# Two more tiles' first products by seven block products, and one table of steps for the whole program

## The chip, the core and the metric

The kernel runs on one core of a Trainium2 chip. The metric is the time of one execution on the device in microseconds (us); lower is better. Engines: PE (matmul; PEld is its weight load), DVE, ACT, POOL, and SP, which here issues all DMAs.

## What is computed

Attention with a window of 128 over 8 batches of 576 tokens and 8 heads, and on its output a dense GELU block:

```python
scores = q @ k.T / sqrt(64) + bias            # bias: -slope * |i - j|
scores = where((0 <= i - j) & (i - j < 128), scores, -1e9)
attn = softmax(scores) @ v                    # 8 x 8 x 576 x 64
x = attn as 4608 x 512
h = x @ w_in                                  # 512 x 2048
g = 0.5 * h * (1 + erf(h / sqrt(2)))
out = g @ w_out                               # 2048 x 512
```

All arrays are float32.

## The kernel before, in words

**Products.** Nearly every float32 operand is split into a high and a low float16 part, and a product is three float16 products (high-high, low-high, high-low). The 4608 tokens are nine tiles of 512. A tile needs its *first product* (h, from x and w_in), GELU, and its *second product* (from g and w_out).

**Plain form.** `mlp_in` (L845) makes h of a tile in 16 banks of PSUM, each by 12 products of 128x128 weights and 512 columns: 192 in all. `mlp_out` (L892; L889 for tile 0, in float32) does as much for the output.

**Block form.** x, w_in and h are seen as two by two blocks, and seven block products of half size (p1 to p7) take the place of eight; some of them use sums of blocks of x (xs) and of w_in (t). With `d` from 0 to 3 for four pieces of 512 features, each piece takes 7 x 12 products of 256 columns: 336 a tile. `Middle` (L1205) does so for tiles 4, 5 and 6, `Seven` (L1093) for tile 8. Both collect the products in two banks, u and v; between products ACT copies u out and DVE adds v to the copy, and GELU follows. `seven_out` (L1302) makes the second products of tiles 7 and 8 in block form too, by sums of g (slots, made in `Sums`) and of w_out (L1318).

**Sums of the weights.** `store_sums` (L982, step K) makes the sums of w_in in eight groups: six POOL ops, a cast by ACT, a low part by DVE, a store to memory (`stored`). It works in the buffers ld_0 and ld_1, which also take q and k of each batch. `load_middle` (L1183) and `load_sums` (L1004) load them again, 1 MB for each piece. `sums_of_weights_out` (L1011, steps P0 to P2, and piece 3 in tile 7) makes the sums of w_out on DVE and ACT into qbuf, kbuf, vbuf and e_main, after attention is done with these.

**Sums of x.** `sums_of_middle` (L1173, step Z) makes them half on POOL and half on DVE.

**Order of the work.** Each function is a generator that issues one or a few instructions at each step. Two tables written out as text set the order for all engines: `ORDER` for batches 0 to 2 and tiles 0 and 1, and after it `LATER` up to tile 6. An engine runs its instructions in that order and waits where an operand isn't ready. Letters name the work: s, S scores; M, N softmax; w, W, y, Y products with v; H and 1 to 7 first products; o, O second products; q, v splitting of q, k and v; a digit ahead is the tile. Tables of bank numbers choose PSUM banks. Between the two tables the pools of PSUM and of the output buffers are closed and opened anew (L1477). Tiles 7 and 8 stand behind the tables as a plain loop (L1531).

**The beginning.** Batch 0's attention is exact float32: scores, softmax on ACT from PSUM, `turn` (PE transposes, L711), `turned` (ACT copies, L719), `weigh` (L798), `leave` (x of tile 0, L818). Beside it ACT and DVE put together and split w_in (`magnitude_in`, `join_in`, `split_in`: L338, L345, L360), and ACT passes once over v for its largest value (`stat_v`, L484), which the scale of x needs.

```python
IN = (4, 5, 6, 8)
...
    with tc.manual_schedule(engines=None):
        for step in ORDER.split():
            next(tasks[step])
...
    early.close()
...
        for step in LATER.split():
            next(later[step])
    for t in range(FAST_OUT, NTILE):
...
        if t == FAST:
            seven_all(t, places)
```

## Time and profile before

| | |
|---|---|
| median of 3 runs | 866.54 us (866.50 to 867.53) |
| profiled execution | 866.36 us |
| its span, first to last instruction | 864.6 us |
| busy PE, DVE, ACT, POOL | 848.4, 696.0, 627.7, 296.9 us |
| mean granted clock of PE | 0.998 |

The span is what the views of the trace cover; about 1.8 us of the execution lie around it. Busy times are of one engine each and overlap. Matmuls are pipelined: the mean of one is longer than the distance from one to the next, which is read from how long a row of them takes.

### The profile page before, as it was taken

What the parts mean: (1) busy time and instruction counts of PE and PEld (TensorE: products, weight loads), DVE (VectorE), ACT (ScalarE), POOL (GpSimd) and SP (SyncE); (2) the same over time, 40 slices, a digit from 0 to 9 for tenths busy, and PEclk for the clock granted to TensorE, in tenths of its full rate; (3) what the DMA queues carried; (4) which work ended last, traced back from release to release, by engine and by line L of the source; (5) the groups of instructions that cost most, each with busy time, mean ns of one, the idle gap of its engine ahead of it and who ended that gap; (6) DMA issues with size and microseconds to landing.
All of it is one profiled execution on the core that took longest, in us unless ns stands there. A gap on an engine that the chain in (4) does not pass through costs nothing.

```text
span 864.6 us, 18999 instructions
## 1 busy us (share of the span) xinstructions
PE 848.4 (98%) x7572; PEld 520.5 (60%) x7572; DVE 696.0 (81%) x1258; ACT 627.7 (73%) x1236; POOL 296.9 (34%) x481
## 2 busy tenths in 40 slices
PE   6999999999999999999999999999999999999998
PEld 4654445544554455445478647865686554588887
DVE  6999999999887865988586989799968899922861
ACT  7999879897678967796579595968596647713850
POOL 2011000123056972879624555547244510000000
PEclk9999999999999999999999999999999999999999
DMA  9865844644542468324943566266712630111201
GB/s 310 278 198 185 291 121 109 161 130 90 124 116 62 105 143 194 98 68 142 231 160 103 186 141 208 81 196 147 213 50 55 119 97 1 49 62 38 98 2 50
DMA packets 178057, 112.64 MB, mean 130 GB/s; under 512 B 134064, under 2 KB 156720, under 8 KB 175792
## 3 DMA queue, kind: packets, MB, share of 16 engines
q1 hardware_dynamic: 177968, 111.43, 44.8%
q8 instruction: 59, 0.97, 0.5%
q14 instruction: 30, 0.25, 0.1%
HBM read 63.31 MB, written 13.63 MB: 89 GB/s over the span
## 4 chain that ended last, share of the span: by engine, by line
PE 75%; DVE 13%; ACT 4%; DMA 4%; issue 3%; POOL 1%; SPq 0%; ACTq 0%; DVEq 0%; POOLq 0%
PE o L892 28%; PE h L845 13%; PE u L1216 7%; PE v L1216 5%; PE av L798 4%; PE u_out L1318 4%; PE sc L617 4%; PE u L1114 2%; PE v L1114 2%; PE z_out L1318 1%; PE x_out L1318 1%; PE y_out L1318 1%; PE v_out L1318 1%; DMA q<-qp 1%; DVE nmax L726 1%
## 5 line engine op out<-in xcount | busy, mean ns | idle before, releaser
L845 PE MATMUL h<-x,wi 128*128 128x512 f16 x960 | 211.2, 379 | 2.1 <-ACT g L866 1.5
L892 PE MATMUL o<-wo,g 128*128 128x512 f16 x864 | 192.2, 379 | 0.0
L892 PEld LDWEIGHTS <-g 128*128 128x128 f16 x1152 | 110.6, 98 | 131.4 <-issue 0.3
L845 PEld LDWEIGHTS <-wi 128*128 128x128 f16 x960 | 92.9, 98 | 115.9 <-issue 5.3
L730 ACT ACTIVATE s<-s,nmax 128x192 f32<-128x192 f32 x252 | 111.5, 444 | 27.3 <-DVE nmax L726 25.3
L740 POOL TENSOR_SCALAR s<-s,z 128x192 f32<-128x192 f32 x180 | 96.0, 554 | 39.2 <-DVE z L734 23.7
L643 DVE SCALAR_TENSOR_TENSOR s<-sc,cs,bias_h 128x384 f32<-128x384 f32 x112 | 67.1, 607 | 3.1 <-PE sc L617 2.7
L649 POOL MEMSET s<- 64x128 f32 (+1 forms) x112 | 19.3, 174 | 143.4 <-DVE s L643 116.4
L892 PE MATMUL o<-wo_first,g 128*128 128x512 f16 x288 | 66.0, 379 | 0.0
L1216 PEld LDWEIGHTS <-t 128*128 128x128 f16 x576 | 56.1, 98 | 6.9
L726 DVE TENSOR_REDUCE nmax<-s 128x5 f32<-128x960 f32 (+1 forms) x56 | 58.1, 1043 | 1.2 <-POOL s L649 1.0
L870 POOL TENSOR_SCALAR g<-g,sg 128x512 f16<-128x512 f32 x48 | 41.4, 871 | 49.8 <-DMA q<-qp 26.6
L749 DVE TENSOR_TENSOR e_main<-s,e_main 128x960 f16<-128x960 f32 (+1 forms) x40 | 46.1, 1158 | 14.8 <-ACT e_main L742 14.5
L889 PE MATMUL o<-zo,g 128*128 128x512 f32 x128 | 57.0, 597 | 0.0
L617 PE MATMUL sc<-kbuf,qbuf 64*64 64x192 f16 (+3 forms) x1656 | 48.8, 251 | 7.8 <-ACT qbuf L518 4.4
L742 ACT CAST e_main<-s 128x960 f16<-128x960 f32 (+1 forms) x40 | 36.1, 908 | 25.0 <-POOL s L740 24.2
L302 DVE SCALAR_TENSOR_TENSOR g<-g,sg,g 128x512 f16<-128x512 f32 x48 | 40.7, 864 | 9.8 <-POOL g L870 9.7
L730 ACT ACTIVATION_READ_ACCUMULATOR s<-s,nmax 128x1 f32 x252 | 47.3, 188 | 0.0
L798 PEld LDWEIGHTS <-vbuf 128*64 128x64 f16 x1392 | 40.1, 111 | 8.7 <-issue 7.7
L1216 PEld LDWEIGHTS <-wi 128*128 128x128 f16 x432 | 42.0, 98 | 5.5
L866 ACT ACTIVATE g<-h,gs 128x512 f32<-128x512 f32 x48 | 31.6, 687 | 15.0 <-PE h L845 7.5
L798 PE MATMUL av<-et,vbuf 128*64 128x128 f16 (+2 forms) x1392 | 42.4, 220 | 0.1
(274 smaller groups left out, 1634.9 us busy)
## 6 DMA issues: line engine op xcount, KB each, us to landing
t<-stored SPq DMA_DIRECT2D x12, 1024.0 KB, 4.9
v<-vp SPq DMA_DIRECT2D x32, 320.0 KB, 5.2
out<-ob SPq DMA_DIRECT2D x34, 256.0 KB, 2.5
raw<-w_in SPq DMA_DIRECT2D x8, 1024.0 KB, 11.2
raw<-w_out SPq DMA_DIRECT2D x8, 1024.0 KB, 8.2
q<-qp SPq DMA_DIRECT2D x7, 1152.0 KB, 5.4
k<-kp SPq DMA_DIRECT2D x7, 1152.0 KB, 8.6
stored<-sums SPq DMA_DIRECT2D x8, 512.0 KB, 2.6
```

Of the source, the lines that this page charges most:

```text
L617: done = nc.tensor.matmul(ps[bank][o, n, gap:W], a, m[:, gap:W], start=(i == 0 and (n == 0 or b > 0)), stop=(i == len(terms) - 1 and b > 0 ...
L643: yield nc.vector.scalar_tensor_tensor(out=s[:, bank[0] : bank[0] + k, :], in0=ps[bank][:, 0:k, 0:W], scalar=cs, in1=bias.broadcast_to([P, ...
L726: yield nc.vector.tensor_reduce(out=nmax[:, r], in_=s[:, r], axis=AX.X, op=ALU.max, negate=True)
L730: yield nc.scalar.activation(s[:, i, :], s[:, i, :], AF.Exp, bias=nmax[:, i : i + 1], accum_out=z[:, i : i + 1])
L740: yield nc.gpsimd.tensor_scalar(to, s[:, i], z[:, i : i + 1], 1.0, op0=ALU.mult, op1=ALU.mult)
L749: yield nc.vector.tensor_tensor(out=e[:, r, 1, c], in0=st.s[:, r], in1=e[:, r, 0, c], op=ALU.subtract)
L798: done = nc.tensor.matmul(av[r, (js[0] - blocks[0]) * QB : (js[-1] + 1 - blocks[0]) * QB], v32s[b][:, hp, kb, r] if b < EXACT else vbuf[:, ...
L845: done = nc.tensor.matmul(ph, wi[n][:, a, cc, k * P : (k + 1) * P], x[:, cc, b, :], start=(i == 0), stop=(i == 3 * NCC - 1),)
L889: done = nc.tensor.matmul(o, g[:, r, c], zo[n][:, n % 2, k * DM : (k + 1) * DM], start=(fc == first), stop=(fc == last))
L892: done = nc.tensor.matmul(o, g[:, r, a, c], wo[n][:, b, k, :], start=(fc == first and i == 0), stop=(fc == last and i == 2),)
L1216: done = nc.tensor.matmul(ps[:, k * HT : (k + 1) * HT], w(a, i)[:, k * P : (k + 1) * P], m(b, i), start=first and n == 0, stop=True, skip_ ...
L1318: nc.tensor.matmul(ps[name][:, tb], f(d, a)[:, k, tb * P : (tb + 1) * P], w(d, b, k), start=first, stop=True, skip_group_check=True,)
```

## The change

Tile 3 takes `Middle` and tile 7 takes the block form as well (a new class `Last`, for tiles 7 and 8, in place of `Sums` and `Seven`): `IN` now has 3 to 8. Step K stands wholly in tile 2's part of the table; its two first adds of each group are DVE's, the other four stay POOL's. The sums of w_out are made by the same function in tiles 3 to 7 (step L, all six adds on POOL), stored (`stored_out`) and loaded into qbuf, kbuf, vbuf and e_main (steps W0 to W3). Tile 7's sums of w_in are loaded into qbuf, kbuf, qbuf again and ld_1; tile 8's into a buffer of x and ld_1 in turn. In tile 2 ACT makes the high half of g in place of POOL. All steps stand in one table, `ORDER`, with those of tiles 7 and 8 (`Outputs` has the second products as steps A to I and what follows them as r1 to r8); the steps of the beginning stand in another order too. Pools are not closed in between. Attention, the second products and the splitting of the inputs keep the kinds and numbers of their instructions; ACT's table loads, which the order brings about, are 36 for 61.

```diff
-IN = (4, 5, 6, 8)
+HIGH_ACT = (2, 3)
+IN = (3, 4, 5, 6, 7, 8)
...
-z0 z0 z0 b b b b s0 z1 z1 s0 z1 m00 x00 m00 m00 s0 m01 z2 x00 x00 x00 x00 z2 n00 m01 z2 z2 F F s1 s1 x01 x01 z n00 n00
+0z0 0z0 0z0 0b 0b 0b 0b 0s0 0z1 0z1 0s0 0z1 0m00 0x00 0m00 0m00 0s0 0m01 0z2 0x00 0x00 0x00 0x00 0z2 0n00 0m01 0z2 0z2
...
-        yield nc.gpsimd.tensor_scalar(g[:, r, 0], g32, gsg[t, n], 1.0, op0=ALU.mult, op1=ALU.mult)
+        if t in HIGH_ACT:
+            yield nc.scalar.activation(g[:, r, 0], g32, AF.Copy, scale=gsg[t, n])
+        else:
+            yield nc.gpsimd.tensor_scalar(g[:, r, 0], g32, gsg[t, n], 1.0, op0=ALU.mult, op1=ALU.mult)
...
-    def store_sums(d, i):
+    def store_sums(d, i, outer):
...
-            yield nc.gpsimd.tensor_tensor(
-                out=r[:, m], in0=b[:, 0, 2 * i : 2 * i + 2], in1=b[:, 1, 2 * i : 2 * i + 2], op=ALU.add
-            )
+            if outer:
+                parts_of = [wo[2 * d + m][:, a, i].rearrange("p (c f) -> p c f", c=2) for a in range(2)]
+            else:
+                parts_of = [wi[2 * d + m][:, a, 2 * i : 2 * i + 2] for a in range(2)]
+            yield (nc.gpsimd if outer else nc.vector).tensor_tensor(out=r[:, m], in0=parts_of[0], in1=parts_of[1], op=ALU.add)
...
-    def sums_of_weights_out(d):
+    def load_sums_out(d):
...
+        if t == FAST_OUT and d < 3:
+            yield load_sums(t, d, spare[d % 2])
+            return
+        if t == FAST and d % 2 == 0:
+            yield load_sums(t, d, flat_of(room([P, NCC, 2, TT], F16, "x", f"t{t}_{d}", 2, t)))
+            return
...
+    class Last(Middle):
...
+        def e(self):
+            yield from self.gelu(self.room(2), self.u)
+            a11, a21, a22 = self.view(0), self.view(2), self.view(3)
+            yield from self.sum(S1, a22, a21, a22, ALU.add)
+            yield from self.sum(S3, a21, a11, a21, ALU.subtract)
+            yield from self.sum(S2, a11, a22, a11, ALU.subtract)
...
-    early.close()
...
-        for step in LATER.split():
+        for step in ORDER.split():
             next(later[step])
-
-    for t in range(FAST_OUT, NTILE):
```

**Order on PE, first product of tile 7.** Before, all 192 products of 512 columns follow the last second product of tile 6:

```order
L892 LDWEIGHTS g_3_8808
L892 MATMUL o_3_9481<-wo_2182,g_3_8808 128x512
L845 LDWEIGHTS wi_510
L845 MATMUL h_0_9685<-x_8128,wi_510 128x512
...
L845 MATMUL h_1_9700<-x_8128,wi_510 128x512
L845 LDWEIGHTS wi_570
L845 MATMUL h_2_9730<-x_8128,wi_570 128x512
```

In the change (x and the first weights of w_in, xs for sums of x, qbuf and kbuf holding sums of w_in; 12 of each kind in a row):

```order
L1080 LDWEIGHTS wi_663
L1080 MATMUL u_1_9875<-x_8323,wi_663 128x256
L1080 LDWEIGHTS qbuf
L1080 MATMUL u_0_9826<-xs_9648,qbuf 128x256
...
L1080 MATMUL v_0_9674<-xs_9648,qbuf 128x256
...
L1080 MATMUL u_0_9826<-x_8323,qbuf 128x256
L1080 LDWEIGHTS kbuf
L1080 MATMUL u_1_9875<-xs_9648,kbuf 128x256
```

Products of 256 columns on several banks (u, v of pieces 0 and 1) stand where 512-column products of one bank after the other stood; between the last product with v that tile 7 needs and the first with sums stand 36 of tile 6's second product and 24 of tile 7.

**Order on ACT, before x of tile 0 leaves.** Here et is the copy of turned weights, x with stv the pass over v, zi and raw the words of w_in, wi its split, the last row the first part of x. Before:

```order
L683 ACTIVATE s_3_390,z_3_391<-sc_3_4_375,nmax_3_387 128x192
L484 ACTIVATE x_440,stv_439<-v_0_200 128x2560
L719 COPY et_2_455<-tp_2_0_444 128x512
L719 COPY et_2_455<-tp_2_2_449 128x512
L719 COPY et_1_329<-tp_1_5_462 128x512
L719 COPY et_1_329<-tp_1_7_470 128x512
L719 COPY et_2_455<-tp_2_4_475 128x256
L360 ACTIVATE wi_510<-zi_259,sww 128x1024
L719 COPY et_2_455<-tp_2_5_479 128x512
L719 COPY et_2_455<-tp_2_7_491 128x512
L818 ACTIVATE x_440<-av_0_0_406,scv_468 128x512
```

In the change:

```order
L742 COPY et_2_454<-tp_2_2_461 128x512
L742 COPY et_2_454<-tp_2_4_467 128x256
L742 COPY et_2_454<-tp_2_5_471 128x512
L742 COPY et_2_454<-tp_2_7_477 128x512
L359 ACTIVATE zi_492<-raw_216 128x1024
L507 ACTIVATE x_502,stv_501<-v_0_204 128x2560
L837 COPY tail<-av_1_1_517 128x64
L381 ACTIVATE wi_523<-zi_374,sww 128x1024
L381 ACTIVATE wi_526<-zi_374,sww 128x1024
L841 ACTIVATE x_502<-av_0_0_415,scv_505 128x512
```

The copies of units 1 and 2 stand ahead of the pass over v instead of behind it; a pass over raw words and a second split of weights stand ahead of the first part of x.

**Order on SP, tiles 7 and 8.** Before, two loads of tile 8's sums stand behind the last results of tile 6:

```order
L753 DMA_TRANSPOSE et_3_9477<-e_main 128x20x128
L753 DMA_TRANSPOSE et_3_9477<-e_main 128x16x128
L906 DMA out<-ob_2_9495 128x512
L906 DMA out<-ob_3_9660 128x512
L1007 DMA room_x<-stored_104 128x4096
L1007 DMA room_9013<-stored_103 128x4096
L1353 DMA out<-ob_0_0_10115 128x2x256
```

In the change (stored is w_in's sums, stored_out w_out's):

```order
L999 DMA vbuf<-stored_out_109 128x4096
L988 DMA stored_out_110<-wsums_1_9822 128x2048
L995 DMA qbuf<-stored_105 128x4096
L999 DMA kbuf<-stored_out_108 128x4096
L995 DMA t_3_10137<-stored_106 128x4096
L927 DMA out<-ob_3_9919 128x512
L999 DMA qbuf<-stored_out_107 128x4096
L995 DMA t_1_10420<-stored_104 128x4096
L999 DMA e_main<-stored_out_110 128x4096
L995 DMA t_0_10577<-stored_103 128x4096
```

Eight loads and a store of sums stand there, and several of them go into a buffer that products of tile 7 still read.

## Rows read from the trace of the kernel before

**Rows 1.** The page's busy times (us, share) and clock by slice.

```profile
PE 848.4 (98%) x7572; PEld 520.5 (60%) x7572; DVE 696.0 (81%) x1258; ACT 627.7 (73%) x1236; POOL 296.9 (34%) x481
...
PEclk9999999999999999999999999999999999999999
```

**Rows 2.** Busy time of each engine by stretch: span, us, then engines, clock, DMA.

```profile
0.00:39.00 39.00, 30.06 (x355) 22.45 (x356) 30.47 (x67) 33.11 (x96) 6.93 (x20) 0.96 0.97 324
39.00:100.00 61.00, 59.53 (x311) 28.25 (x313) 58.69 (x80) 58.50 (x73) 6.11 (x6) 1.00 0.55 194
...
251.40:346.40 95.00, 93.48 (x789) 46.10 (x788) 68.98 (x123) 77.35 (x134) 62.58 (x90) 1.00 0.51 123
346.40:442.10 95.70, 95.70 (x824) 47.83 (x823) 75.29 (x129) 67.99 (x131) 72.78 (x98) 1.00 0.50 142
442.10:530.50 88.40, 88.40 (x934) 60.42 (x933) 76.88 (x139) 64.81 (x132) 46.93 (x74) 1.00 0.51 149
...
709.30:750.70 41.40, 41.40 (x194) 18.84 (x193) 39.48 (x59) 31.69 (x48) 0.00 (x0) 1.00 0.02 7
...
787.40:864.60 77.20, 73.36 (x672) 65.51 (x670) 41.52 (x63) 37.57 (x59) 0.00 (x0) 1.00 0.12 44
```

**Rows 3.** PE's waits: for whom, us in total, times, longest.

```profile
PE sc L617 <- ACT qbuf L518: 4.4, 1, 4.4
PE tp L711 <- ACT et L719: 2.0, 1, 2.0
PE h L845 <- ACT g L866: 1.5, 1, 1.5
```

**Rows 4.** The chain in order of time: start, us, engine, line, instructions.

```profile
367.18 23.42 PE h L845 x108
...
555.38 2.62 PE u L1216 x24
...
709.28 41.44 PE h L845 x192
```

**Rows 5.** A group of PEld: busy us, mean ns of one, idle before.

```profile
L1216 PEld LDWEIGHTS <-t 128*128 128x128 f16 x576 | 56.1, 98 | 6.9
```

**Rows 6.** Groups of ACT, DVE and POOL by line and shape.

```profile
L730 ACT ACT_TABLE_LOAD x29 | 37.2, 1283 | 0.5
L866 ACT ACTIVATE g<-h,gs 128x512 f32<-128x512 f32 x48 | 31.6, 687 | 15.0 <-PE h L845 7.5 <-DVE g L302 7.2
L1258 ACT COPY rooms<-u 128x512 f32<-128x512 f32 x24 | 13.9, 580 | 9.0 <-PE u L1216 8.8
L1259 DVE TENSOR_TENSOR rooms<-v,rooms 128x512 f32<-128x512 f32 x24 | 16.5, 688 | 10.3 <-PE v L1216 5.2 <-ACT rooms L1258 5.1
L968 DVE TENSOR_TENSOR room<-wo 128x1024 f32<-128x1024 f16 x6 | 7.3, 1215 | 0.0
L989 POOL TENSOR_TENSOR sums<-wi 128x512 f32<-128x512 f16 x16 | 25.9, 1626 | 36.0 <-DVE qbuf L302 35.7
```

**Rows 7.** First adds (POOL) and low parts (DVE) of w_in's sums, first and last start.

```profile
L989 POOL TENSOR_TENSOR sums<-wi x16: 1148/1300/3462, 245.0 to 402.5; 128x512 f32<-128x512 f16 x16
...
L999 DVE TENSOR_TENSOR sums<-sums x8: 1211/1238/1839, 257.9 to 409.9; 128x1024 f16<-128x1024 f32 x8
```

**Rows 8.** DMA issues: KB each, median us to landing.

```profile
t<-stored SPq DMA_DIRECT2D x12, 1024.0 KB, 4.9
```

**Rows 9.** PE in order of time, 30 to 39 us: start, us, group, idle before.

```profile
32.44 1.93 PE L711 MATMUL tp<-ident,e_main 128*128 128x128 f32 x8 [1.99 <-ACT et L719]
...
38.95 0.39 PE L845 MATMUL h<-x,wi 128*128 128x512 f16 x1
```

**Rows 10.** ACT in order of time, 29 to 38 us.

```profile
29.21 2.60 ACT L484 ACTIVATE x<-v 128x2560 f16<-128x2560 f32 x1
...
35.69 1.03 ACT L818 ACTIVATE x<-av,scv 128x512 f16<-128x512 f32 x1
```

**Rows 11.** Busy times and clock of one us behind the hole.

```profile
33.00:34.00 1.00, 1.00 (x7) 1.00 (x6) 1.00 (x3) 1.00 (x4) 0.00 (x0) 0.50 1.06 393
```

More of the change, by code (lines that the diff above doesn't have):

```diff
@@ L1356, in seven_out @@
-        copies = [2, 5, 2]
-        one, two = (features(0, 0), weights(0, 0)), (features(1, 0), weights(1, 0))
-        add("u", *one, every[:last])
-        if rest:
-            rest.p4()
-        yield
-        add("u", *one, every[last:])
-        c1 = copy("u")
-        if rest:
-            rest.p3()
-        yield
-        if rest:
-            add("x", features(1, 1), sum_of_weights(T4), every)
-            yield
-        add("v", *two, every)
-        leave("v", c1, 0, 0)
-        yield
@@ new lines, in leave @@
+        def leave(self, names, n, tok, half):
+            ob = room([P, 2, DM // 2], F32, "ob", f"ob{self.t}_{tok}_{half}", 3)
+            rows = out[self.t * TT + tok * HT : self.t * TT + (tok + 1) * HT, half * (DM // 2) : (half + 1) * (DM // 2)]
+            rows = rows.rearrange("(b p) f -> p b f", p=P)
+            for name, tb in zip(names, (slice(0, 2),) if len(names) == 1 else (slice(0, 1), slice(1, 2))):
+                yield self.plus(ob, name, n, tb)
+                yield nc.sync.dma_start(rows[:, tb], ob[:, tb])
```

767 lines of the change are left out of this document (333 added, 434 removed).

## The prediction

> **What bounds the kernel now.** I read the page's busy shares first: PE is busy 848.4 of 864.6 us, at nine tenths of full clock or more in every slice [rows 1]. That alone could be an average over unlike stages, so the stretches of the program come next [rows 2]: from 39 us on PE misses 1.47 us in 39 to 100, 1.52 in the stage of tile 2, nothing in those of tiles 3 and 4 and in tile 7's first product, and 3.84 in the last stretch, where the last result is still scaled and stored. In the first 39 us it misses 8.94. These make 15.8 of the 16.2 us that PE does not work. The view of PE's waits names the causes: 4.4 us until the first inputs are there, 2.0 for a copy by ACT in batch 0's attention, 1.5 for tile 2's GELU [rows 3]. DVE and ACT are near full too, but only until 205 us: in 39 to 100 DVE works 58.69 and ACT 58.50 of 61 us, and still PE works 59.53 [rows 2]. So the end is set by the sum of PE's instructions, plus some 12 us at the two ends and some 4 us of waits between. An edit is worth what it takes from PE's instructions, as long as it makes no new wait.
>
> **The products.** For tile 7, 192 products of 512 columns stand in a row, 41.44 us, 215.8 ns each; in tile 3 a piece of 108 took 23.42, 216.9 ns each [rows 4]. The block form, as tiles 4 to 6 run it, took 2.62 us for 24 products of 256 columns, 109.2 ns each [rows 4]. In the new order exactly two tiles change form: the 512-column products of that line fall from 960 to 576, and those of 256 columns in all block forms rise from 1344 to 2016. Removed: 2 x 192 x 216.3 ns (the middle of the two rows) = 83.1 us. Added: 672 x 109.2 ns = 73.4 us. The gain is **9.7 us**, or 9.5 by tile 7's row alone; I take 9.6. The second products of all tiles keep form and number.
>
> Each of those 256-column products needs its own weight load, and there are 288 more of them. A load has a mean of 98 ns [rows 5], under the 109.2 ns of a product, and the pitch of 109.2 was measured with these loads beside it, so they cost nothing more. The Trainium skill speaks against the change here: TensorE: Matmul & The Clock Gate, section Back-to-back issue gap, gives a stream of weight load and matmul 131 ns per matmul at 512 columns and 81 at 128. On a straight line between them, about 98 ns at 256 (my estimate from that page), it would make the two tiles 672 x 98 - 384 x 131 = 15.6 us dearer. The rows have 216 and 109 in place of 131 and 98, what the same section's formula for matmuls in isolation gives, so I go by the rows.
>
> **Other engines' work in tiles 3 and 7.** Tile 3 gains 12 copies on ACT (580 ns) and 12 adds on DVE (688 ns) [rows 6], 7.0 and 8.3 us. Its stage has 27.7 us of ACT and 20.4 of DVE free [rows 2], less 4.8 us of PE time that goes. Tile 7's new work is that of tile 8, where 77.2 us hold 41.52 of DVE and 37.57 of ACT [rows 2]. Two such tiles now follow each other over some 147 us. On average all of this is covered; what can fail is one result that comes late (second rival).
>
> **The sums of w_in, now all in tile 2.** They were spread over tiles 2 and 3 [rows 7]. Their 16 first adds leave POOL (1626 ns) for DVE; the nearest DVE row is an add of twice the size, 1215 ns [rows 6], so 16 x 0.61 = 9.7 us, and four more groups bring 4 x 1.24 = 5.0 of low parts [rows 7]. With the second half of tile 3's sums of x (by its neighbours some 6 us) DVE comes to 69.0 + 20.7 = about 90 of the stage's 95 us. Tile 2's 16 high halves move from POOL to ACT at about 0.69 each, the mean of a like GELU: 11 us onto 77.35. ACT gets room elsewhere: the new order has 36 table loads for 61, and each of the 25 has 1283 ns [rows 6], 32 us over the program. DVE at 90 of 95 is no denser than the 58.7 of 61 beside which PE hardly stood still [rows 2]; I cost it at nothing. The bounds are nothing and 5 us, if DVE's excess over nine tenths were all to reach PE.
>
> **The wait for tile 2's GELU.** The 1.5 us [rows 3] came where GELU needs a free buffer, which DVE frees after POOL's high half. With ACT making that half, POOL and its queue leave the loop. Bounds: no gain, and 1.5; I take 0.8, since DVE's part stays.
>
> **The sums of w_out.** 33 us of DVE work late in the program go (8 adds at 1215 ns [rows 6] and 32 ops of half that size); 16 adds at 1626 ns and 32 smaller ones go to POOL in tiles 3 to 6, which has 23 and 41 us free in tiles 3 and 4 [rows 2], plus 8 stores and 4 loads. They are off the path. What they add is in the queue of SP: each load of sums into qbuf, kbuf, vbuf and e_main waits for the last reader of that buffer, and everything behind it on SP waits too. The shortest lead is the load into qbuf of the last third of tile 7: in the order on PE five products of 12 stand between the buffer's last reader and its first use, 5 x 12 x 109.2 ns = 6.6 us; such a load took 4.9 us from issue to landing [rows 8]. Behind it on SP are the next tables, whose users stand ten products and more further on. Covered by 1.7 us; bounds nothing and 3 us.
>
> **The beginning.** Until PE's first h product at 38.95 us [rows 9] ACT is the fullest engine, 33.11 of 39 [rows 2]. PE waited 1.99 us for the copies of turned weights [rows 9], behind ACT's pass over v of 2.6 us from 29.21 [rows 10]; after that hole the granted clock was 0.50 [rows 11], the 1.2 GHz level. In the new order all copies of units 0 to 2 stand ahead of that pass, so this wait goes. But next late is x: the first h product needs its first part, which ACT left from 35.69 [rows 10], and now one more pass over raw words and one more split of weights stand ahead of it, about 2.1 us, of which ACT's own short waits give back up to 1.5. So h begins between 0.8 us earlier and 0.8 later, and a hole right ahead of h may put its first products on the lower clock: 3 us at half speed, 1.5 us lost. The other end is the whole of it gained, 2.0 + 1.5 = 3.5. I take nothing, as ACT's sum of work up to there is the same.
>
> **The sum.** The profiled execution took 866.36 us, its span 864.6. 866.4 - 9.6 - 0.8 = **856.0 us**; the median of the runs, 866.54, is 0.2 above the profiled one, within what the runs differ.
>
> **The rivals.**
> *First, a better beginning.* The hole and the lower clock go and nothing takes their place, and with them part of the other waits: 856.0 - 3.5 to - 7, so 849 to 852.5. For it: 4.5 us of the first 39 are neither start nor work. Against: ACT has 33 us of work there. Chance 0.10.
>
> *Second, new short waits in tiles 7 and 8.* The first sums product of tile 8 needs a bank that ACT must first have copied, into a buffer that two DVE results of tile 7 have to leave. In the order on PE 3.9 us stand between (36 products), and the chain has two ACT ops of 0.6 to 0.7 and two DVE ops of 0.7 [rows 6], 2.7 us without the hops and with DVE's queue empty. Places like this and the load above, five or six at 1 to 1.5 us each, cost 3.5 to 9: 859.5 to 865. Against: in tile 8 before PE never waited. Chance 0.13.
>
> *Third, on the other side: tile 3's tables come too late.* The eight groups ran from 245.0 to 411 us, 20.8 us each, not for their work but because each stands in the queues of POOL, ACT and DVE behind attention, and uses a buffer in turn with the loads of q and k [rows 7]. They can't start sooner, since q and k of batch 3 hold the buffers until then. At that pace the last is stored 59 us after tile 3's first sums product is due, some 6 us into its stage at 346.4; at half that delay PE, with some 5 us of other products left, would stand for 20 to 30 us: 876 to 886. It decides from a standstill of 10.4 us up. Against: their own work is some 9 us a group, two groups can overlap, and q's splitting alone made 35.7 us of POOL's waits there [rows 7]; the new order has the groups close together behind it. Chance 0.04. Beside it stands a second way to the same side: the 288 more weight loads come into the open, 288 x 98 ns = 28.2 us [rows 5], 884; the pitch in tiles 4 to 6 speaks against it [rows 4], chance 0.01. The skill's rule above would give such a result, by 15.6 us.
>
> *No change*, every us given back at other places: chance 0.02.
>
> **How the numbers follow.** My case, everything within 3.5 us of the sum, has 0.70: 852.5 to 859.5. The range is 852 to 861: it takes in that, an edge of the first rival and half of the second. About 0.2% (1.7 us) is what a measurement of this kernel can tell from no change. Faster by more: 0.70 + 0.10 + 0.13 = 0.93; same 0.02; slower 0.05.
>
> **What would show it.** PE's busy time near 838.8 us and 288 more matmuls; h only in tiles 0 to 2; no hole of PE in tiles 3 and 7 above half a us; the stage of tile 3 about 91 us. Of the beginning: no wait on copies at 30 us, the first h product between 38.2 and 39.8. I am wrong if the pitch of 256 columns in tile 7 is not 109 ns, if PE waits on t or sums, or if the first 39 us gave more than 3 us either way.

## The result, and the profile after

The changed kernel took 876.56 us, the median of 4 runs (875.57 to 877.09), beside 866.52 (865.62 to 867.53) for the one before on the same chip: a ratio of 1.011, 95% interval 1.0093 to 1.0127. It is slower by 10 us; I had forecast 856.0 us and a range of 852 to 861. The profiled execution took 877.01 us, its span 875.2.

The page of after, busy times and PE's granted clock by slice:

```profile
PE 840.9 (96%) x7860; PEld 548.6 (63%) x7860; DVE 721.4 (82%) x1278; ACT 621.7 (71%) x1248; POOL 321.3 (37%) x509
...
PEclk9989999999999999999999999999999999999999
```

PE has 288 more matmuls and is busy 7.5 us less than in [rows 1]. But it now stands still for 875.2 - 840.9 = 34.3 us, where it stood for 16.2. The next view says where: busy time of each engine by stretch (span, then PE, PEld, DVE, ACT, POOL, clock, DMA), first of before and then of after.

```profile
39.00:60.00 21.00, 20.79 (x136) 10.85 (x135) 20.18 (x34) 20.44 (x34) 2.89 (x3) 1.00 0.40 123
60.00:140.00 80.00, 78.56 (x441) 36.24 (x440) 76.19 (x131) 70.78 (x124) 6.18 (x19) 1.00 0.59 194
140.00:350.00 210.00, 208.33 (x1863) 105.07 (x1862) 174.91 (x362) 170.21 (x342) 87.48 (x128) 1.00 0.50 124
350.00:650.00 300.00, 299.91 (x2967) 194.35 (x2966) 248.09 (x439) 222.48 (x439) 168.48 (x265) 1.00 0.51 146
650.00:760.00 110.00, 110.00 (x899) 61.46 (x897) 100.69 (x160) 71.73 (x145) 24.96 (x48) 1.00 0.26 59
```

```profile
39.00:60.00 21.00, 15.07 (x93) 8.44 (x94) 18.68 (x39) 16.81 (x30) 1.63 (x2) 0.84 0.01 2
60.00:140.00 80.00, 80.00 (x464) 37.29 (x462) 77.42 (x121) 72.52 (x127) 7.35 (x19) 1.00 0.67 214
140.00:350.00 210.00, 206.53 (x1842) 104.29 (x1842) 187.87 (x391) 167.77 (x348) 80.71 (x126) 1.00 0.53 136
350.00:650.00 300.00, 288.40 (x3019) 198.88 (x3013) 257.90 (x440) 209.53 (x428) 172.26 (x263) 1.00 0.58 156
650.00:760.00 110.00, 108.85 (x1071) 78.32 (x1069) 80.03 (x125) 66.96 (x140) 53.74 (x82) 1.00 0.50 139
```

Two stretches carry it. In 39 to 60 us PE misses 5.93 us for 0.21, and runs its first products at a granted clock that brings the mean there to 0.84. In 350 to 650, tiles 3 to 6, it misses 11.6 us for 0.09. The view of PE's waits in after (for whom, us in total, times, longest):

```profile
PE av L821 <- DMA et<-e_main: 9.2, 6, 2.4
PE h L868 <- DVE x L323: 6.1, 1, 6.1
PE sc L640 <- DMA kbuf<-kp: 4.4, 1, 4.4
...
PE u L1080 <- DVE xs L1013: 1.2, 1, 1.2
```

The third row is the start, as in [rows 3]. The second is the first h product; it starts at 44.93 us (38.95 in [rows 9]). The fourth of the rows shown is a wait for sums of x (`xs`) at 729 us. The first is new: in attention the transposed softmax weights (`et`, loaded by DMA from `e_main`) come late. PE in order of time, 500 to 650 us (start, us, group, idle before):

```profile
517.15 1.59 PE L821 MATMUL av<-et,vbuf 128*64 128x128 f16 x60 [1.83 <-DMA et<-e_main]
538.25 1.59 PE L821 MATMUL av<-et,vbuf 128*64 128x128 f16 x60 [2.35 <-DMA et<-e_main]
...
631.42 1.54 PE L821 MATMUL av<-et,vbuf 128*64 128x128 f16 x42 [2.44 <-DMA et<-e_main]
```

The load itself is hardly slower: its median from issue to landing is 4.2 us, and 4.1 before. What it waits for, the softmax on POOL, ACT and DVE, is late. In before PE never waits for `et` in these stages.

Against my sum the profiled execution has 21.0 us too many: 2.1 of PE busy time (840.9 for 838.8) and 18.9 of PE idle time (34.3 for 15.4). By stretch the idle part is 5.7 in 39 to 60, 11.5 in 350 to 650, 2.6 in 140 to 350 (with the 0.8 that I had taken off), 1.2 in 650 to 760, and less than before in 60 to 140 (-1.4) and at the end (-0.7).

### The profile page after: what moved, and what is told of

Its sections match the earlier page's. It is cut to its first block, busy times and chain, and to the rows that moved or that the text cites. A ratio compares the mean times of both kernels' runs of the same rounds, so it can differ in the third digit from the quotient of the medians.

```text
span 875.2 us, 19688 instructions
## 1 busy us (share of the span) xinstructions
PE 840.9 (96%) x7860; PEld 548.6 (63%) x7860; DVE 721.4 (82%) x1278; ACT 621.7 (71%) x1248; POOL 321.3 (37%) x509
## 4 chain that ended last, share of the span: by engine, by line
PE 48%; DVE 25%; ACT 8%; DMA 5%; issue 5%; POOL 4%; SPq 0%; DVEq 0%; ACTq 0%; POOLq 0%
PE u L1080 11%; PE v L1080 9%; PE h L868 7%; PE o L913 7%; PE u_out L1230 4%; DVE s L666 3%; DMA k<-kp 3%; DVE nmax L749 3%; ACT s L753 2%; PE av L821 2%; DVE g L323 2%; POOL s L763 2%; PE o L910 2%; DMA et<-e_main 2%; DVE e_main L772 1%
## 5 line engine op out<-in xcount | busy, mean ns | idle before, releaser
L868 PE MATMUL h<-x,wi 128*128 128x512 f16 x576 | 129.6, 383 | 7.2 <-DVE x L323 6.1
L763 POOL TENSOR_SCALAR s<-s,z 128x192 f32<-128x192 f32 x180 | 104.6, 597 | 33.3 <-DVE z L757 28.7
L1080 PEld LDWEIGHTS <-t 128*128 128x128 f16 x1008 | 98.5, 98 | 12.5 <-issue 0.6
L868 PEld LDWEIGHTS <-wi 128*128 128x128 f16 x576 | 56.2, 99 | 75.6 <-issue 9.1
L1080 PEld LDWEIGHTS <-wi 128*128 128x128 f16 x864 | 83.9, 98 | 13.6 <-issue 1.6
L666 DVE SCALAR_TENSOR_TENSOR s<-sc,cs,bias_h 128x384 f32<-128x384 f32 x112 | 65.4, 608 | 3.2 <-PE sc L640 2.3
L772 DVE TENSOR_TENSOR e_main<-s,e_main 128x768 f16<-128x768 f32 (+1 forms) x40 | 51.7, 1298 | 14.0 <-ACT e_main L765 13.4
L1080 PE MATMUL u<-xs,t 128*128 128x256 f16 x504 | 60.5, 273 | 0.2
L821 PE MATMUL av<-et,vbuf 128*64 128x64 f16 (+2 forms) x1392 | 42.9, 220 | 11.2 <-DMA et<-e_main 9.2
L1131 POOL TENSOR_SCALAR g<-rooms,sg 128x512 f16<-128x512 f32 x48 | 39.8, 834 | 37.3 <-ACT rooms L1125 30.1
L765 ACT CAST e_main<-s 128x768 f16<-128x768 f32 (+1 forms) x40 | 36.0, 906 | 18.3 <-POOL s L763 13.3
L323 DVE SCALAR_TENSOR_TENSOR g<-rooms,sg,g 128x512 f16<-128x512 f32 x48 | 39.5, 841 | 5.4 <-POOL g L1131 5.4
## 6 DMA issues: line engine op xcount, KB each, us to landing
raw<-w_in SPq DMA_DIRECT2D x8, 1024.0 KB, 10.8
```

The source lines that it names most:

```text
L323: return nc.vector.scalar_tensor_tensor(out=dst, in0=src, scalar=scale, in1=high, op0=ALU.mult, op1=ALU.subtract)
L666: yield nc.vector.scalar_tensor_tensor(out=s[:, bank[0] : bank[0] + k, :], in0=ps[bank][:, 0:k, 0:W], scalar=cs, in1=bias.broadcast_to([P, ...
L763: yield nc.gpsimd.tensor_scalar(to, s[:, i], z[:, i : i + 1], 1.0, op0=ALU.mult, op1=ALU.mult)
L772: yield nc.vector.tensor_tensor(out=e[:, r, 1, c], in0=st.s[:, r], in1=e[:, r, 0, c], op=ALU.subtract)
L821: done = nc.tensor.matmul(av[r, (js[0] - blocks[0]) * QB : (js[-1] + 1 - blocks[0]) * QB], v32s[b][:, hp, kb, r] if b < EXACT else vbuf[:, ...
L868: done = nc.tensor.matmul(ph, wi[n][:, a, cc, k * P : (k + 1) * P], x[:, cc, b, :], start=(i == 0), stop=(i == 3 * NCC - 1),)
```

## The experiments

My theory after this: the beginning has a cause of its own, and the sums of w_out, now made in tiles 3 to 6, delay the softmax there. The rivals: the second is the shadow of the first, or lies with the order on PE, or with one overfull engine.

### The hole at 39 us: POOL's first maximum

POOL in order of time from 12 to 40 us, after:

```profile
30.28 0.63 POOL L678 MEMSET e_main<- 128x640 f16 x1 [19.15 <-PE tp L734]
37.14 0.37 POOL L288 PARTITION_ALL_REDUCE stw<-stw  x1 [6.22 <-issue]
```

and the instructions of that line in its queue:

```profile
L288 POOLq MODIFY_POOL_CONFIG  x2: 11/11/11, 30.9 to 30.9; - x2
```

The maximum over partitions that gives the scale of w_in's first two parts had the second of its inputs from DVE at 33.86 us and ran at 37.14, 6.2 us after POOL's setting for it (`MODIFY_POOL_CONFIG`). In the new order POOL's clearing of `e_main` (step 0cl) stands ahead of the maximum and waits for PE till 30.28, so the setting, which stands behind it, starts only then. Before, only the scaling of q stood ahead, done at 12.5 us, and the setting ran while POOL had no work:

```profile
L267 POOLq MODIFY_POOL_CONFIG  x2: 7/7/7, 12.4 to 12.5; - x2
```

This agrees with the Trainium skill, GPSIMD Engine Reference, section Instruction dispatch: the first call after such a setting pays some 6 us (5.95 measured there) for loading code, with no instruction in the profile. In after DVE then waits 2.37 us for `stw`, ACT's split of w_in 2.29 for DVE, and PE's first h 6.05 for x.

**e1_clear** moves the clearing behind the maximum:

```diff
-0t2 0cl 0t2 0e2 0t2 0e2 0e2 0a1 0p0 0j1
+0t2 0t2 0e2 0t2 0e2 0e2 0a1 0p0 0cl 0j1
```

> The changed kernel with one step moved in the beginning: the clearing of e_main on POOL stands behind the first maximum over partitions of the weights, as it did before the change, and no longer ahead of it. Theory A (POOL's custom code): in the changed kernel the setting of POOL for that maximum came at 30.9 us, behind the clearing that waits for PE, and the maximum started 6.2 us later with nothing else to wait for; before the change the setting was done at 12.4 us, while POOL was idle. Then the maximum should start near 33.9 us, when DVE has its input, the first h product near 39 instead of 44.93, and the whole should be 6 to 8 us shorter (868.5 to 870.5): 6.0 of waiting and up to 2.0 of products on the lower clock. Theory B (ACT and DVE have more work ahead of the first x, the place of the maximum is only a symptom): 0 to 2 us shorter.

**e2_warm** keeps the order and takes an early maximum over a new tile of 8 bytes, so that the setting runs at the start. **e5_warm64** does so with 64 bytes, **e10_warm0** over a tile that was there, so that no address moves (the code shown is e2's). **e11_shift** puts 64 unused bytes ahead of all tiles of the kernel *before*.

```diff
+    warm = pool.tile([P, 2], F32, name="warm")
...
+        yield nc.gpsimd.partition_all_reduce(warm, warm, P, bass_isa.ReduceOp.max)
```

> The changed kernel with one instruction more: a maximum over partitions of a small tile of zeros on POOL, right behind the scaling of q, at some 11 us; the clearing of e_main stays ahead of the real maximum. Theory A (what was late is the setting of POOL, some 6 us before its first custom instruction): as with the clearing moved, 6 to 8 us shorter, 868.5 to 870.5. Theory C (the maximum is late because it stands in POOL's queue behind a clearing that waits for PE): no gain, 876.5, since the clearing stays where it is; it ended at 30.9, three us before the maximum's input.

> The kernel with the early maximum on POOL once more, its small tile now 64 bytes a partition instead of 8. Theory H (the run with the 8-byte tile lost 5.6 us against the changed kernel although its first h product came 1.85 us earlier, because that tile moved e_main and all behind it from a multiple of 64 bytes to 32 past one: its transposed loads out of e_main took 5.0 us in the median, least 4.2, instead of 4.2 and 3.7): with 64 bytes the transposes are back at 4.1 to 4.2, PE's waits for them at 5 to 10 us instead of 14.0, and the whole is 873 to 875.5. Theory I (the early maximum itself, or the earlier first product, upsets the later stages): again 880 or more.

> The kernel with the early maximum on POOL a third time, now over a tile that is there already, so that no address changes. Theory A (the setting of POOL is what was late): first h product near 43.1 as in the two forms before. Theory H2 (those two lost 5 us and more because the added tile moved e_main off a multiple of 512 bytes, by 32 and by 64, and its transposed loads took 4.9 to 5.0 us for it): transposes 4.1 to 4.2 us again, least 3.6 to 3.7, and the whole 873 to 875, as with the clearing moved. Theory I (the early maximum itself upsets the later stages): transposes as short, and still 879 to 882.

> The kernel before the change, with a tile of 64 bytes put in front of all others, so that e_main and the rest lie 64 bytes further on; nothing else is changed. Theory H2 (place of e_main): transposes of 4.9 us in place of 4.1. Theory O (before the change these transposes had slack, the changed order has none): PE waits for them no more than 1 us in all, and the time is 866 to 868, against the 3 to 6 us that the same move cost the changed kernel. If they had no slack here either: 870 to 873.

e1 took 873.33 us (1.0086, 1.0064 to 1.0108), e10 873.46 (1.0073, 1.0044 to 1.0102): some 3 us less than after, though the intervals overlap with after's. POOL in e1 has no wait on its setting any more:

```profile
34.29 1.42 POOL L285 PARTITION_ALL_REDUCE stw<-stw  x1 [22.87 <-DVE zi L357]
```

Yet h begins at 43.51 there and at 43.28 in e10, 1.4 to 1.65 us earlier, not six: PE still waits about 4 us for x. POOL's setting is a part of the hole, not the whole of it. Another part is on DVE: the maximum's second input, which DVE makes from the words of w_in, itself came 10.8 us later than before, and all that needs the scale comes behind it. DVE and POOL in before, and DVE in after:

```profile
21.88 1.21 DVE L339 TENSOR_SCALAR_CACHE_REDUCE zi<-zi 128x1024 f32<-128x1024 f32 x1
23.23 0.38 POOL L267 PARTITION_ALL_REDUCE stw<-stw  x1 [10.77 <-DVE zi L339]
```

```profile
32.64 1.21 DVE L360 TENSOR_SCALAR_CACHE_REDUCE zi<-zi 128x1024 f32<-128x1024 f32 x1
```

In e1 the maximum is still 11 us later than before (34.29 for 23.23).

e2 (882.16) and e5 (881.74) came out 8 to 9 us *over* e10 with the same early maximum, and e11 (873.76; 1.0082, 1.0051 to 1.0113) 6.6 us over the kernel before with no edit but the shift. So it is the addresses. The loads `et<-e_main` between 140 and 720 us, least, median and greatest time to landing, first e10 and then e5 and e11:

```profile
DMA to landing us min/median/max: 3.6/4.2/7.6
```

```profile
DMA to landing us min/median/max: 4.2/4.9/7.8
```

```profile
DMA to landing us min/median/max: 4.3/5.0/8.4
```

`e_main` begins at byte 35840 of a partition, a multiple of 512, in before, after and e10; 32 bytes on in e2 (5.0 us median) and 64 in e5 and e11. Each transposed load takes 0.7 to 0.8 us longer there, and PE's waits for them are 14.0 us in e2 and 15.4 in e5, for 7.9 in e10. The place of the loads' destination moves too, but one of the two destinations begins at byte 111392 in before and in e2 alike, and the least time of a load is 3.6 us in before and 4.2 in e2; so it is the source's place that counts. The direction is that of the Trainium skill, DMA: Bandwidth & Descriptors, section How a descriptor splits into AXI transactions: a descriptor that does not start at a multiple of 256 bytes fetches from the boundary below and takes more. That this is the mechanism for transposed loads no run here shows; only these three places of the source were compared.

### The rest of the beginning

**e7_first** and **e9_first2** put the parts of ACT's and DVE's work that x needs ahead of the second split of weights (in e7 one step stood so that ACT idled 2.5 us; e9 mends it). **e13_oldbegin** takes before's order for the first 240 steps, with PSUM banks chosen for it. The order in e1 and in e9:

```diff
-0p0 0cl 0j1 0p0 0p0 0F 0z 0a2 0j1 0p0 0p0 0a2 0m31 0m31 0v0 0v0 0F 0W2 0v0
+0p0 0cl 0j1 0p0 0p0 0F 0z 0v0 0p0 0p0 0v0 0F 0W2 0v0
...
-0i0 0i0 0i1 0i1 0t3
+0i0 0i0 0t3
-0l0 0l0 0w2 0w1 0l1 0l1 0d 0l2 0l2 0a4 0a4
+0l0 0l0 0w2 0w1 0l1 0l1 0j1 0i1 0i1 0d 0l2 0l2 0a2 0a2 0m31 0m31 0a4 0a4
```

> The kernel with the clearing of e_main moved, and in the beginning four steps more: ACT's pass over v goes ahead of the pass over the third part of the words of w_in, and that part's two steps, the second joining of words and the maxima of unit 3 go behind the scaling of the first three units' results. Theory B2 (what is left of the late first h product after the clearing is moved, 43.51 against 38.95 us before the change, is this work standing ahead of the first x on ACT and DVE): the first h product at 39.5 to 41, 2.5 to 4 us shorter than with the clearing alone (873.3), 869 to 871. Against it: the moved work is late for what follows at 45 to 60 us, where ACT and DVE are full: then the gain at the first h product comes back as waits there, and the whole is 872 to 874.

> The kernel with the changed beginning, mended: in the last form ACT stood 2.5 us in front of the second split of weights, which waits for the joining of words that had been moved behind on DVE, and the three parts of x stood behind that split. Now the second joining, and the splits that need it, stand behind the first two parts of x. Theory B2 again (the first h product is late by the work ahead of the first x): first h product at 39.3 to 40.5 in place of 43.38 and 44.93; if the later stages follow it, 870 to 872. Theory N (the later stages are paced by POOL, ACT and DVE, which do not gain what PE gains in the beginning): the first h product as early, the whole at 873 to 875.

> The changed kernel with the first 240 steps of its order as they stood before the change (up to the fifth h product's start), the rest as it is now; the PSUM banks of these steps are given out anew. Theory R (the new beginning as a whole, not the first h product alone, is what costs: PE missed 17.3 us up to 250 us against 10.8 before, and of these 6.5, with 2.0 of products on the lower clock, moving POOL's clearing gave back 3): PE misses 10 to 12 us up to 250 us and the whole is 6 to 8.5 us shorter than the changed kernel, 868 to 870.5. Theory S (up to 230 us DVE and ACT set the pace whatever the order, so a better beginning is worth 3 us at most): 873 to 875.

e7 took 875.28 (h at 43.38), e9 875.72 (1.0084, 1.0055 to 1.0112): neither is told from e1 or from after. PE in e9:

```profile
40.34 2.11 PE L868 MATMUL h<-x,wi 128*128 128x512 f16 x9 [2.02 <-DVE x L323]
45.29 1.11 PE L734 MATMUL tp<-ident,vbuf 128*128 128x128 f32 x4 [2.84 <-DVE x L323]
```

h came 4.6 us earlier, but what had been put off for it was missing at 45 us. Here an earlier first product by itself gained nothing that the runs can tell. In 60 to 140 us of after DVE works 77.42 of 80 us and ACT 72.52; that work put off to there stays late is my reading, and no run tests it. e13 took 871.48 (8 runs; 1.0057, 1.0042 to 1.0073), 5.1 us less than after. Its span is 6.8 us shorter: 5.0 of PE idle time (29.3 for 34.3) and 1.8 of busy time, since h no longer starts on the lower clock. The new beginning costs 5 us, some 3 of them by POOL's queue. e13 puts everything back at once, DVE's maxima too (POOL's first maximum runs at 23.59 there), so where the other 2 us come from is not settled.

### The waits in tiles 3 to 6: the sums of w_out

**e3_nosums** makes no sums of w_out, **e14_neither** is e13 without them.

```diff
 def store_sums(d, i, outer):
+    if outer:
+        for _ in range(7):
+            yield
+        return
...
-        yield nc.sync.dma_start(spare[d][:, 0:4096], stored_out[d].rearrange("p i a n f -> p (i a n f)"))
+        yield nc.sync.dma_start(spare[d][:, 0:4096], stored[d].rearrange("p i a n f -> p (i a n f)"))
```

> The changed kernel without the making of the sums of w_out in tiles 3 to 6 (their adds, copies, subtractions and stores are left out; tiles 7 and 8 load the sums of w_in in their place). Theory D (the 9.2 us for which PE waits for the transposed weights of attention in tiles 3 to 6 come from this work, which stands in POOL's, ACT's and DVE's queues ahead of attention's): these waits fall to under 2 us, and the whole is 7 to 9 us shorter, 867.5 to 869.5. Theory E (they come from the order of attention's own steps and of the splitting of q and k, and from POOL and DVE slowing each other): 0 to 3 us shorter.

> The kernel with the old beginning and without the making of the sums of w_out (left out as before: tiles 7 and 8 load the sums of w_in in their place). If the beginning and these sums are the two causes and add up: 8 us shorter than with the old beginning alone, 860 to 862.5; what then still lies above the forecast of 856.0 are the waits of tiles 3 to 5 that come from neither. If they share the same waits: 863 to 868.

e3 took 868.61 (10 runs; 1.0019, 1.0002 to 1.0035), 8.0 us less than after; e14 864.57 (10 runs; 0.9975, 0.996 to 0.9991), 6.9 less than e13. That is short of the 8 that I had set for two causes that simply add up: e14 lies 12.0 us under after, where 5.1 and 8.0 make 13.1. The stretch 350 to 650 in e13 and then in e14:

```profile
350.00:650.00 300.00, 289.92 (x3044) 202.13 (x3042) 256.50 (x449) 211.77 (x435) 174.17 (x268) 1.00 0.60 160
```

```profile
350.00:650.00 300.00, 294.53 (x3071) 205.62 (x3069) 249.38 (x445) 208.13 (x432) 138.61 (x235) 0.99 0.56 149
```

So the hole in tiles 3 to 6 is not the shadow of the beginning: a better beginning leaves 10.1 us of it, and without the sums 5.5 are left. The two runs leave out all of the sums' work at once, POOL's adds, ACT's casts, DVE's low parts and the stores; the loads stay. POOL works 174 of 300 us in e13, far from full; DVE works 256.5, and 7.1 us less without the sums. Which part of the work costs has to be read in the queues. Before the wait at 517 us, POOL, ACT and DVE in after:

```profile
502.27 0.70 POOL L1131 TENSOR_SCALAR g<-rooms,sg 128x512 f16<-128x512 f32 x1
502.93 0.43 POOL L763 TENSOR_SCALAR s<-s,z 128x192 f32<-128x192 f32 x1
503.64 0.84 POOL L763 TENSOR_SCALAR s<-s,z 128x192 f32<-128x192 f32 x1 [0.27 <-DVE z L757]
...
505.74 0.99 ACT L765 CAST e_main<-s 128x960 f16<-128x960 f32 x1 [1.43 <-POOL s L763]
...
499.62 2.80 DVE L391 TENSOR_REDUCE stv<-v 128x1 f32<-128x2560 f32 x1
...
507.19 1.37 DVE L987 TENSOR_TENSOR wsums<-wsums 128x1024 f16<-128x1024 f32 x1
...
508.55 0.94 DVE L749 TENSOR_REDUCE nmax<-s 128x4 f32<-128x768 f32 x1
509.41 2.01 DVE L772 TENSOR_TENSOR e_main<-s,e_main 128x960 f16<-128x960 f32 x2
```

From 497 to 502.3 POOL had made five instructions of a group of sums, with softmax work (L763) behind them. But they are not what ACT's cast of `e_main` waited 1.43 us for: POOL itself then waited for DVE, 0.27 us for `z` and 0.29 for `s`, ahead of the last scaling that the cast needs. DVE has no gap here from 496 to 511 us. Its pass over v of 2.80 us stands ahead of `z`; and when the cast ended at 506.73, DVE still took 1.37 us for the sums' low part ahead of the `nmax` and the `e_main` that the load needs, against PE's wait of 1.83. So at this place the delay is in DVE's queue, and the low part is most of it. The same was not worked out for the other places.

DVE and POOL also slow each other. The longest of DVE's `e_main` instructions ran beside an add that POOL had begun a little earlier:

```profile
431.26 2.90 DVE L772 TENSOR_TENSOR e_main<-s,e_main 128x960 f16<-128x960 f32 x1
```

```profile
431.03 2.12 POOL L1004 TENSOR_TENSOR xr<-x 128x1024 f32<-128x1024 f16 x1
```

POOL's end, 433.15, and the 1.15 us that is the median of this line of DVE make 434.3; it ended at 434.16. The Trainium skill, SBUF — State Buffer, section SBUF: two separate sides, says just this: a DVE instruction with two inputs from SBUF and one of POOL that reads SBUF lock each other out for the whole instruction, and the first to start goes on. The mean of the 20 of this form went from 1224 ns before to 1433, but it is 1432 in e14 too: it is a part of what remains there, not of what the sums of w_out cost. What it may cost PE is seen in e14; DVE, POOL and PE there:

```profile
521.24 4.33 DVE L772 TENSOR_TENSOR e_main<-s,e_main 128x768 f16<-128x768 f32 x2 [0.39 <-issue]
```

```profile
521.03 2.13 POOL L1008 TENSOR_TENSOR xr<-x 128x1024 f32<-128x1024 f16 x1 [3.04 <-DVE x L323]
```

```profile
530.79 2.54 PE L821 MATMUL av<-et,vbuf 128*64 128x128 f16 x60 [2.00 <-DMA et<-e_main]
```

Two `e_main` instructions took 4.33 us, where two such made without POOL's adds beside them take 0.94 and 1.15; the load follows them, and PE waits 2.00 us, the longest of e14's waits in these tiles. The same place has 4.33 us and PE's wait of 2.35 in after, at 528.97 and 538.25. No run moves POOL's add away. In before, too, one such instruction took 2.01 us beside POOL's add, at 516.91, and PE did not wait.

**Who makes them, and when.** **e4_kpool** gives the first adds of w_in's sums in tile 2 back to POOL, **e6_ldve** gives those of w_out's to DVE; **e15_late** is e13 with three quarters of w_out's sums made in tile 7 on POOL; **e16_high** is e13 with the high halves of g in tiles 3 to 6 on ACT and no longer on POOL, **e17_high2** the same for the last two of four pieces only.

```diff
-yield (nc.gpsimd if outer else nc.vector).tensor_tensor(out=r[:, m], ...)
+yield nc.gpsimd.tensor_tensor(out=r[:, m], ...)     # e4
+yield nc.vector.tensor_tensor(out=r[:, m], ...)     # e6
...
+later[f"W{d}"] = late_sums_out(d) if d else load_sums_out(d)     # e15
...
-yield nc.gpsimd.tensor_scalar(g[:, :, 0], v, sg, 1.0, op0=ALU.mult, op1=ALU.mult)
+yield nc.scalar.activation(g[:, :, 0], v, AF.Copy, scale=sg)     # e16; e17 only if self.d > 1
```

> The changed kernel with the 16 first adds of the sums of w_in on POOL again, all other steps as they stand. Theory F (DVE at 87.4 of 101 us in tile 2 makes the short waits there, 1.2 us at 231 and 1.1 at 273.8): up to 2.3 us shorter. Theory G (these adds are covered on DVE, and on POOL they stand in the way of attention's scaling, 1.6 us each): the same or up to 4 us longer.

> The changed kernel with the 16 first adds of the sums of w_out on DVE, as those of w_in are, instead of POOL; the 32 small ones stay on POOL. Theory J (the sums of w_out cost 8 us because POOL is slow at them and is in the chain of attention: a first add took 1.4 to 1.5 us there, and attention's scaling stands behind it): 2 to 6 us shorter, and PE's waits for the transposed weights fall below 5 us. Theory K (DVE, which works 83 to 87 of 95 to 100 us in these stages, is the engine without room, and any work more on it costs PE as much): the same to 8 us longer.

> A version meant to be faster than both kernels: the old beginning, and of the sums of w_out only a quarter made in tile 3 and stored, as now; three quarters are made in tile 7 on POOL, which has no work there, straight into the buffers that hold them, with their copies and subtractions on ACT and DVE. If the sums cost 8 us only because of where they stand: 5 to 6 us of them go, 862.5 to 865. If POOL's sums slow DVE in tile 7, or come late for the second product: up to 5 us back, 865 to 870.

> The kernel with the old beginning; in addition ACT makes the high half of each result of tiles 3 to 6, 16 a tile, in place of POOL (some 0.7 us each on either). Theory T (in tiles 3 to 6 the pace is set by POOL's queue, in which these halves and the sums of w_out stand ahead of attention's scaling, and by POOL and DVE slowing each other): POOL has 11 us a tile less, PE's waits between 350 and 650 us (10.1 with the old beginning) fall to 5 to 7, 866 to 869. Theory U (it is the queue of ACT or DVE: ACT, at 195 of 278 us there, gets 11 us a tile more, with attention's exponentials behind them): 871 to 877.

> As the last one, but ACT makes only the high halves of the third and fourth part of each tile, 8 a tile; these stand among attention's steps, those of the first two parts stand where POOL has little to do. Theory T: nearly the same gain as with all 16, or more, 865 to 869. Theory U: half its loss, 871 to 874.

None gained. e4 took 882.74 (1.0188, 1.0172 to 1.0204), 6.2 us over after: DVE was the right place for tile 2's adds. e6 took 879.81 (1.0151, 1.0125 to 1.0177), 3.3 over after: with POOL relieved by 12 us in 350 to 650 (159.9 for 172.3) and DVE at 261.3 us for 257.9, PE misses 13.5 us there for 11.6. That speaks for theory K, in which DVE has no room, more than for J. But DVE's load alone does not make the waits: e14 has DVE at 249.4 us and misses 5.5, before had it at 248.1 and missed 0.09. e16 took 887.01, 15.5 over e13 and beyond what either theory had set; PE waits for ACT's copies between products now:

```profile
PE u L1080 <- ACT rooms L1121: 7.2, 5, 2.4
```

e17 took 872.77, 1.3 over e13 and within what the runs differ; theory T had set 865 to 869. e15 took 887.11, 15.6 over e13, far beyond its 862.5 to 870. Its three last stretches from 350 us on:

```profile
350.00:650.00 300.00, 295.04 (x3096) 206.96 (x3095) 253.56 (x450) 210.91 (x435) 155.60 (x249) 1.00 0.58 153
650.00:760.00 110.00, 95.80 (x916) 64.80 (x914) 75.13 (x112) 59.15 (x127) 69.27 (x93) 0.97 0.34 89
760.00:887.00 127.00, 119.30 (x1066) 105.38 (x1064) 79.20 (x119) 60.23 (x92) 3.38 (x4) 0.97 0.17 61
```

Tiles 3 to 6 lose 5.0 us for e13's 10.1, about what they lose without the sums (5.5 in e14), which bears out that the sums are the cause there; but in 650 to 760 PE misses 14.2 for 1.2. Made in tile 7 on POOL they cost more than in tiles 3 to 6. An order that makes them early and costs nothing was not found.

**The order of steps.** **e8_later** moves four steps of second products on PE ahead of the weighing that waits for `et`; **e18_later13** is e13 with the same moves; **e12_both** is e9 with the softmax steps of tiles 3 to 5 earlier in ACT's and DVE's queues. The first move of e8, then that of e12 in tile 3:

```diff
-3Y3 ... 3o3
+3o3 3Y3 ...
...
-3N30 3v 3v 3X1 ... 3M31 ... 3N30 ... 3N31 3N31
+3M31 3N30 3N30 3N31 3N31 3v 3v 3X1 ...
```

> The changed kernel with four steps of second products on PE (3.5 us each) moved ahead of the products of attention weights and v of the last unit of tiles 3, 4 and 5, and of the second unit of tile 4, where PE waited 1.4, 2.35, 2.4 and 1.8 us for transposed weights; no other engine's order changes. Theory L (these waits are a matter of PE's order: there is other work for PE at hand): up to 8 us shorter, 869 to 872. Theory M (the chain through POOL, ACT and DVE is what paces these stages, and PE waits for its end in any case): the waits go to the next place that needs the results, the sums of x or the next tile's first products, and the whole stays at 875 to 877.

> The kernel with the mended beginning, and in tiles 3 to 5 some steps of attention's last units moved forward on ACT and DVE: copies of weights ahead of an x that waits for its scale, subtractions behind them at once and ahead of the scales of q and k, one group's last step of the sums of w_out behind them. No work is added or left out. Theory P (the waits of tiles 3 to 5 come from these few places in ACT's and DVE's queues, where a short step stands behind one that waits): PE's waits for transposed weights fall from some 9 us to under 4, and the whole is 3 to 6 us shorter than with the mended beginning alone. Theory Q (the three engines together have no room there, and what moves forward moves something else back): within 1.5 us of it.

> e13 (before's order of the beginning) with the same moves as e8: four steps of second products stand on PE ahead of the weighing of attention's values in tiles 3, 4 and 5, where PE waited for transposed loads. In e8's profile the stretch from the first product of tile 3 to the sums product of tile 6 at 644 us was 2.8 us shorter than in the changed kernel, but a wait in tile 2, ahead of the moved steps, came 0.9 us longer and the clock fell behind it, 2.6 us in all, and the median did not move. Theory: the order on PE around the weighing is a part of what is left in tiles 3 to 6, and e8's tile 2 is apart from it; then this runs 2 to 4 us under e13's 871.5, at 867.5 to 869.5, and the waits in 350 to 650 us fall from 10.1 to about 6. Rival: what PE doesn't wait for there it waits for at the next place, as DVE and POOL are late whatever PE does; then 870.5 to 872.5.

e8 took 876.84 and e18 870.82 (1.0051, 1.0036 to 1.0066), the time of after and of e13. The waits for `et` fall, to 2.6 us from 9.2 in e8 and to 1.9 from 6.3 in e18, and the waits for DVE grow. In e18:

```profile
PE v L1077 <- DVE s L663: 2.3, 3, 1.2
PE sc L637 <- DVE x L320: 2.1, 4, 1.1
```

For these e13 has 1.3 us once, and no such `sc` row. The moves do take idle time off: in 350 to 650 PE misses 7.2 us for 11.6 in e8 and 7.4 for 10.1 in e18:

```profile
350.00:650.00 300.00, 292.58 (x3044) 202.30 (x3043) 256.31 (x447) 211.18 (x434) 173.16 (x266) 1.00 0.60 160
```

But PE's busy time in the profiled executions grows as much, to 844.6 from 840.9 us in e8 and to 842.3 from 839.1 in e18. In e18 2.1 us of that are products with k (`sc`), which follow each other less closely; in e8 1.8 are h products of tile 2 on the lower clock. So the place on PE moves the delay more than it removes it. e12 took 879.01 (1.014, 1.0106 to 1.0173), 3.3 over e9: its waits for `et` were to fall under 4 us and are 7.0; one load came 3.70 us late, and the granted clock fell behind it. Of 18 kernels none but e14, which leaves work out, took less than the kernel before.

## Why the prediction was wrong

**The products: right.** PE busy was to be 838.8 us and was 840.9. Some 2 us are lower clock: in 44.9 to 48.9, behind the hole of 6.05 us, it is 0.50, the 1.2 GHz level, and nine h products take 4.00 us there, where the 216 ns of [rows 4] make 1.94:

```profile
44.90:48.90 4.00, 3.97 (x10) 1.53 (x10) 3.93 (x8) 3.99 (x11) 0.00 (x0) 0.50 0.00 0
```

e13, whose h products run at 1.00, has 839.1. In tile 7 groups of 12 stand 1.31 us apart, 109.2 ns a product as taken from tiles 4 to 6; the weight loads stayed hidden. The rule of the Trainium skill (TensorE: Matmul & The Clock Gate, Back-to-back issue gap) does not agree with these rows either:

```profile
733.04 1.47 PE L1080 MATMUL v<-xs,qbuf 128*128 128x256 f16 x12
734.35 1.47 PE L1080 MATMUL u<-x,qbuf 128*128 128x256 f16 x12
```

**"They are off the path" failed.** I put the sums of w_out at nothing, bounds nothing and 3 us, and of all their work I priced only the loads on SP. They measured 6.9 (e13 to e14) and 8.0 us (after to e3). The loads weren't it: they stay in e3 and e14, and PE waits for none of them. I had taken POOL's 23 and 41 free us in tiles 3 and 4 as cover, and not asked whose softmax stands behind each group in POOL's, ACT's and DVE's queues. The sum does not even name the eight casts on ACT and eight low parts on DVE that go with the adds, though I had counted four such low parts at 5.0 us for w_in; DVE works 257.9 us in 350 to 650 with the sums (after) and 251.1 without (e3). The 33 us of DVE that it takes off late in the program are 29 by the sizes that it gives; nothing hangs on them.

**The beginning, "I take nothing", failed.** Bounds were a gain of 3.5 and a loss of 1.5; it lost 5.1 (e13). I reasoned on ACT's sum of work and did not read POOL's queue, where the clearing had moved ahead of the maximum (some 3 of the 5.1 us), nor DVE's, where the maxima of w_in had moved behind other work; the first h was to come at 38.2 to 39.8 and came at 44.93. Of the wait on copies [rows 9] 0.24 us are left, but 1.14 us of the same kind came at 32.68, ahead of a product with v.

**"On average all of this is covered" failed by its first two words.** The stage of tile 3, first product to first product of the next, took 93.2 us (352.76 to 445.94) for the 91 forecast and 95.7 before [rows 2], since holes of up to 1.4 us stand in it; I had expected none over half a us. With both causes out e14 is still 8.6 us over 856.0, its profiled execution (865.71 us) 9.7. Of these 5.4 are waits in 350 to 650, 2.2 waits in 140 to 350, 1.3 and 0.9 in 39 to 60 and ahead of it, and 2.0 PE busy time; 2.1 were gained in 60 to 140 and at the end. What makes the waits is not settled. For the longest, 2.00 us, POOL's add beside DVE's `e_main` was read above, but not tested; e8, e12 and e18 show only that moving a few steps gains no time.

**The wait for tile 2's GELU**, -0.8: its row is gone, but at 273.76 us h now waits 1.12 us for DVE (`s`, L666), so 0.4 of the 1.5 was gained. **The sums of w_in** I took at nothing: 140 to 350 lost 1.8 us, inside my bounds of nothing to 5, whether for them or for other causes no run tells; e4 shows that POOL would have been dearer.

**The rivals.** The side was the third's, not its mechanism: PE waits nowhere for tables of w_in (`t`), and no weight load came into the open. The second has one wait, 1.15 us for xs at 729 us, gone without the sums of w_out (e3, e14). My chance of 0.05 for slower rested on those two mechanisms alone, and neither was what happened.

## What to carry to other kernels

Busy shares do not say that added work is covered: for each moved or added instruction look at what stands behind it in its engine's queue and when PE needs that; here eight groups of sums, whose adds stood on an engine with 40% free, cost 7 to 8 us, and in the place that was read it was DVE's small share of them that PE waited for. When steps are reordered, read every queue, the lightest engine's too: one clear in front of POOL's first custom instruction moved its 6 us of setting out of idle time, which cost some 3 us. Before crediting an experiment's edit, see that no buffer changed its address.

## What I had not expected of the hardware

- A shift of 32 or 64 bytes of the source of transposed loads cost 0.7 to 0.8 us of 4.2 in each load, and 6.6 us in the time of an otherwise unchanged kernel (e11, ratio 1.0082).
- POOL's first maximum over partitions came 6.2 us after its setting, without any row in the profile for that time.
- After waits of 4.36 us (e1) and 6.05 us (after) PE's first products ran at a granted clock of 0.55 and 0.50, 9 of them in 3.60 us in e1; after one of 3.99 us 9 took 2.11 us in e5 but 3.52 in e10. The length of a wait alone did not decide it.
